# An FFT and a two-layer network in one kernel: the moving operands of both layers read by halves in turn

## The chip, the cores and the metric

The kernel runs on one core of a Trainium2 chip. The metric is the device time of one execution in microseconds. The kernel before takes 1714.6 us, the median of three runs (1714.3 to 1715.34). TensorE (PE in the profile) multiplies: a product streams the columns of its moving operand past weights that were loaded ahead (PEld), and leaves its result in PSUM. VectorE (DVE), ScalarE (ACT) and GpSimd (POOL) do the elementwise work; SyncE (SP) issues the DMAs.

## The reference

```python
X = np.fft.fft(x, axis=1)            # x: (8, 3008, 256) float32
X = np.fft.fft(X, axis=2)
x = X.real.astype(np.float32).reshape(24064, 256)
h = x @ w_in                         # (256, 2048)
r = np.maximum(h, 0.0)
g = s * (r * r) + b
return g @ w_out                     # (2048, 256)
```

## The kernel before, in words

The transform along the sequence is a set of products with cosine and sine tables, folded so that 1506 columns of each of the 8 samples are kept (`NK`), in three blocks of 502 (`NT`, `NBLK`). The transform along the features is folded into the first weights. Every float32 operand of a large product is split into a high part that is rounded to the format `F32R` and a low part, the rest; a product of two operands is then three products: high by high, high by low and low by high.

A step is one block and one group of 128 of the 2048 hidden features, so there are 8 x 3 x 16 = 384 steps.

- `first_layer` (L673) makes the hidden values of a step: for each of two kinds (the even and the odd part in the features) three products of 502 columns, L679, with `spec_h` or `spec_l` as the moving operand, into a PSUM tile `ab` of two banks. VectorE then adds the row `ebc` times `wny` (L681), and forms difference and sum of the two kinds (L682, L683), so that `h` holds the values for a column and for its mirror. ScalarE does the relu (L684) and the square (L685) in place, and rounds to `gh` (L692). GpSimd (in eleven of the first sixteen steps VectorE) forms `gl` = `h` - `gh` (L695).
- `second_layer` (L698) adds a step into the four PSUM banks `po`: for each of the two halves of `h` three products for each of two halves of the 256 outputs, twelve in all, L705, with `gh` or `gl` as the moving operand. In the first block the moving operand has two more columns, which are ones, so that the column sums of `w_out` come out for the bias. `finish` (L708) scales the four banks (L722) and stores them after 16 steps.

So a step has 6 + 12 products of 502 columns, and the kernel 384 x 18 = 6912 of them. Each has its own weights of 128 by 128. The transform's products (L599) and the weights' and edge column's (L338, L478) are the rest of TensorE's work.

The order of the work is written out by hand in two lists of letters, `START` for the beginning and `BATCH` for each later sample: `L` is a `first_layer`, `S` a `second_layer`, the other letters are pieces of loading, transform and weights. `_in_order` holds every engine to the order in which its instructions were written. `spec`, `gh`, `gl` and `h` have three buffers each and `ab` has two.

The order in which a block's 502 columns stand in memory is free: the host gets from `_columns` which column of the output is which, and puts them where they belong.

Of the kernel before, what the change touches and what calls it, by code (L numbers as in the profile page):

```python
# [9 lines left out]
F32 = mybir.dt.float32  # L10
# [3 lines left out]
ALU = mybir.AluOpType  # L14

P = 128
# [8 lines left out]
NT = 502  # L25
NBLK = 3
# [70 lines left out]
def _quarters(ph):  # L97

    m = _residues(ph)
    n = H // 4 if ph else Q // 4  # L100
    return np.stack([m, n - m, 2 * n - m, n + m], axis=1)


def _columns():

    ks, turned = [], []
    for ph in range(2):
        m = _quarters(ph)
        n = H if ph else Q
        both = np.stack([m, n - m], axis=1)  # L110
        sg = np.stack([_SIGMA, -_SIGMA])[None, :, :, None] + 0 * both
        k = both * (1 if ph else 2)
        k, sg = k.reshape(4, 8, G), sg.reshape(4, 8, G)
        if ph == 0:
            parts = [
                (0, lambda v: v.reshape(2, 4 * G)[:, :-1]), (1, lambda v: v.reshape(4, 2 * G)[:, :-1]),
                (2, lambda v: v), (3, lambda v: v[:, :-1]),
            ]
        else:
            parts = [(0, lambda v: v), (3, lambda v: v), (1, lambda v: v[:, :-1]), (2, lambda v: v[:, :-1])]  # L120
        for r, cut in parts:
            ks.append(cut(k[r]).ravel())
            turned.append(cut(sg[r]).ravel() < 0)
    return np.concatenate(ks), np.concatenate(turned)


def _dft_tables():
# [123 lines left out]
def kernel(ctx: ExitStack, tc: tile.TileContext, xq, xn, dft, turn, feat, w_in, w_out, s, b, out):  # L251
    nc = tc.nc
# [14 lines left out]
    def two_banks():  # L267
        return ps_ab.tile([P, 2, 512], F32, name="ab")
# [14 lines left out]
    wny = const.tile([P, NJ], F32, name="wny")  # L283
# [214 lines left out]
    def block_of(su, blk):  # L498
        if (su, blk) not in spec_tiles:
            spec_tiles[su, blk] = [spec.tile([P, 2, NT], F32R, name=f"spec_{part}") for part in "hl"]  # L500
        return spec_tiles[su, blk]
# [168 lines left out]
            yield  # L670


    def first_layer(su, blk, j, ebc):  # L673
        mh, ml = block_of(su, blk)
        ps = two_banks()[:, :, :NT]
        fj = slice(j * P, (j + 1) * P)
        for kind in range(2):
            for i, (w, m) in enumerate(((wd_h, mh), (wd_h, ml), (wd_l, mh))):
                nc.tensor.matmul(ps[:, kind], w[:, kind, fj], m[:, kind], start=i == 0, stop=i == 2)  # L679
        h = act.tile([P, 2, NT], F32, name="h")  # L680
        nc.vector.scalar_tensor_tensor(h[:, 0], ebc, wny[:, j:j + 1], ps[:, 0], op0=ALU.mult, op1=ALU.add)  # L681
        sub(h[:, 1], h[:, 0], ps[:, 1])  # L682
        add(h[:, 0], h[:, 0], ps[:, 1])  # L683
        nc.scalar.activation(h, h, AF.Relu)  # L684
        nc.scalar.activation(h, h, AF.Square)  # L685
        gh = act.tile([P, 2, NT + 2], F32R, name="gh")
        gl = act.tile([P, 2, NT + 2], F32R, name="gl")
        if (su, blk) == (0, 0):

            nc.gpsimd.memset(gh[:, 0, NT:].bitcast(F32), 1.0)  # L690
            nc.gpsimd.memset(gl[:, 0, NT:].bitcast(F32), 0.0)
        nc.scalar.copy(gh[:, :, :NT], h)  # L692
        yield gh, gl
        engine = nc.vector if su == blk == 0 and j in LOWS_OF_STEPS_ON_VECTOR else nc.gpsimd
        engine.tensor_sub(gl[:, :, :NT], h, gh[:, :, :NT].bitcast(F32))  # L695
        yield

    def second_layer(po, j, g, sums):  # L698
        gh, gl = g
        start, stop = j == 0, j == NJ - 1  # L700
        for pm in range(2):
            n = NT + 2 if sums and pm == 0 else NT
            for l, r, first, last in ((wo_h, gh, True, False), (wo_l, gh, False, False), (wo_h, gl, False, True)):
                for dh in range(2):
                    nc.tensor.matmul(  # L705
                        po[2 * pm + dh][:, :n], l[:, j, dh * P:(dh + 1) * P], r[:, pm, :n],
                        start=start and first, stop=stop and last,
                    )  # L708

# [76 lines left out]
    po = None  # L786
    ebc = None
    step = 0

    def first():  # L790
        nonlocal ebc, step
        su, blk, j = step // (NBLK * NJ), step // NJ % NBLK, step % NJ
        step += 1
        if j == 0:
            ebc = small.tile([P, NT], F32, name="ebc")
            for ph in range(2):
                first, last = max(0, blk * NT - SPLIT * ph), min((blk + 1) * NT - SPLIT * ph, e_dram[ph].shape[1])
                if first < last:
                    at = first + SPLIT * ph - blk * NT
                    nc.sync.dma_start(  # L800
                        ebc[:, at:at + last - first], e_dram[ph][su, first:last].partition_broadcast(P)
                    )
        lows.append(first_layer(su, blk, j, ebc))
        pending.append(((su, blk, j), next(lows[-1])))

    def second():
        nonlocal po
        (su, blk, j), g = pending.pop(0)
        if j == 0:
            po = [ps_o.tile([P, 512], F32, name="po") for _ in range(4)]  # L810
        second_layer(po, j, g, (su, blk) == (0, 0))
        if j == NJ - 1:
            finish(su, blk, po)
# [67 lines left out]
```

## Time and profile before

| | |
|---|---|
| median of three runs | 1714.6 us |
| span of the profiled execution, first to last instruction | 1712.9 us |
| TensorE busy | 1674.9 us, 98% of the span |
| VectorE busy | 1403.5 us, 82% |
| ScalarE busy | 1284.6 us, 75% |
| GpSimd busy | 935.4 us, 55% |
| granted TensorE clock, mean of the span | 0.996 of 2.4 GHz |

The profiled execution has no time of its own beside its span; the median of the runs lies 1.7 us above the span, which is what lies around the first and the last instruction. Products are pipelined: the duration that the profile gives for one holds time in which the next already runs, so what one product costs is read from the distance between the starts of successive ones, not from its duration.

### The profile page before, as it was taken

The numbers are of one execution on the slowest core, as the hardware profiler recorded it, in microseconds if no ns is written. First come the engines' busy times: TensorE is split into PE (matmuls) and PEld (weight loads), VectorE is DVE, ScalarE is ACT, GpSimd is POOL, SyncE is SP. The second block draws the span as 40 slices with busy tenths as digits, with TensorE's granted clock in tenths as the row PEclk, the third lists the DMA queues.
The fourth block names the chain that finished last, engine by engine and source line by source line (L and its number), as shares of the span: only waits on it lengthen the run. The fifth ranks groups of instructions, "written<-read, shape, count | busy, mean of one in ns | idle before, by whom it ended". The sixth has DMA issues, their size and how long they took to land.

```text
span 1712.9 us, 21686 instructions
## 1 busy us (share of the span) xinstructions
PE 1674.9 (98%) x7585; PEld 1382.3 (81%) x7585; DVE 1403.5 (82%) x2134; ACT 1284.6 (75%) x1357; POOL 935.4 (55%) x562
## 2 busy tenths in 40 slices
PE   4899999999999999999999999999999999999998
PEld 3678888788888888888888888888888888888887
DVE  7998989898778978799787997879878897875453
ACT  3877777677787777877877778777878777787776
POOL 5645555555555555655556556555565555565554
PEclk9899999999999999999999999999999999999999
DMA  7421201120001100021000200002000110000000
GB/s 184 111 63 59 64 23 31 29 76 31 1 31 53 52 31 2 30 77 29 31 7 34 77 25 25 31 23 73 22 19 30 44 43 31 1 31 30 2 24 25
DMA packets 25570, 68.56 MB, mean 40 GB/s; under 512 B 4915, under 2 KB 9875, under 8 KB 25366
## 3 DMA queue, kind: packets, MB, share of 16 engines
q1 hardware_dynamic: 24934, 64.83, 12.4%
q0 software_dynamic: 528, 2.36, 0.6%
q8 instruction: 59, 0.97, 0.2%
q14 instruction: 49, 0.40, 0.1%
HBM read 42.45 MB, written 24.73 MB: 39 GB/s over the span
## 4 chain that ended last, share of the span: by engine, by line
PE 89%; DVE 6%; ACT 3%; issue 1%; DMA 1%; POOL 0%; SPq 0%; DVEq 0%; ACTq 0%; POOLq 0%
PE po L705 57%; PE ab L679 28%; PE ab L599 3%; DVE h L681 1%; DVE h L682 1%; DMA raw<-in_w_in 1%; DVE h L683 1%; ACT h L685 1%; PE ab L338 1%; ACT h L684 1%; ACT gh L692 1%; DVE xt L512 0%; DVE cs L517 0%; PE ab L478 0%; POOL gl L695 0%
## 5 line engine op out<-in xcount | busy, mean ns | idle before, releaser
L695 POOL TENSOR_TENSOR gl<-h,gh 128x1004 fp32r<-128x1004 f32 x373 | 817.9, 2193 | 707.9 <-ACT gh L692 488.6
L684 ACT ACTIVATE h<-h 128x1004 f32<-128x1004 f32 x384 | 400.3, 1042 | 350.6 <-DVE h L683 336.0
L705 PE MATMUL po<-gh,wo_h 128*128 128x502 f32 (+1 forms) x1536 | 479.9, 393 | 0.3 <-DVE o L722 0.2
L705 PE MATMUL po<-gl,wo_h 128*128 128x502 f32 (+1 forms) x1536 | 475.1, 391 | 0.7 <-POOL gl L695 0.4
L705 PE MATMUL po<-gh,wo_l 128*128 128x502 f32 (+1 forms) x1536 | 475.3, 391 | 0.0
L681 DVE SCALAR_TENSOR_TENSOR h<-ebc,wny,ab 128x502 f32<-128x502 f32 x384 | 281.3, 733 | 234.5 <-PE ab L679 221.8
L685 ACT ACTIVATE h<-h 128x1004 f32<-128x1004 f32 x384 | 401.3, 1045 | 12.2
L692 ACT CAST gh<-h 128x1004 fp32r<-128x1004 f32 x384 | 397.4, 1035 | 12.6 <-PE po L705 0.3
L705 PEld LDWEIGHTS po<-gl,wo_h 128*128 128x128 f32 x1536 | 290.5, 189 | 61.5 <-POOL gl L695 1.7
L705 PEld LDWEIGHTS po<-gh,wo_l 128*128 128x128 f32 x1536 | 289.1, 188 | 61.3
L705 PEld LDWEIGHTS po<-gh,wo_h 128*128 128x128 f32 x1536 | 286.6, 189 | 59.8 <-DVE o L722 2.7
L679 PE MATMUL ab<-spec_h,wd_h 128*128 128x502 f32 x768 | 303.2, 395 | 7.3 <-ACT spec_h L564 3.7
L679 PE MATMUL ab<-spec_h,wd_l 128*128 128x502 f32 x768 | 300.1, 391 | 0.0
L679 PE MATMUL ab<-spec_l,wd_h 128*128 128x502 f32 x768 | 299.2, 390 | 0.0
L683 DVE TENSOR_TENSOR h<-h,ab 128x502 f32<-128x502 f32 x384 | 260.6, 679 | 13.2
L682 DVE TENSOR_TENSOR h<-h,ab 128x502 f32<-128x502 f32 x384 | 260.2, 678 | 13.3
L679 PEld LDWEIGHTS ab<-spec_h,wd_h 128*128 128x128 f32 x768 | 145.8, 190 | 42.8 <-DVE h L683 9.3
L679 PEld LDWEIGHTS ab<-spec_l,wd_h 128*128 128x128 f32 x768 | 145.8, 190 | 29.2 <-POOL spec_l L566 0.5
L679 PEld LDWEIGHTS ab<-spec_h,wd_l 128*128 128x128 f32 x768 | 144.6, 188 | 30.0
L599 PE MATMUL ab<-dft_sb,fh 96*128 96x192 f32 (+1 forms) x288 | 65.8, 306 | 18.3 <-ACT fh L577 18.3
L722 DVE TENSOR_SCALAR o<-po,sb_s,bias 128x502 f32<-128x502 f32 x94 | 68.8, 794 | 10.4 <-PE po L705 10.4
L512 DVE TENSOR_TENSOR xt<-xt 96x512 f32<-96x512 f32 x56 | 73.4, 1311 | 0.0
(103 smaller groups left out, 960.1 us busy)
## 6 DMA issues: line engine op xcount, KB each, us to landing
xt<-in_xq SPq DMA_DIRECT2D x64, 384.0 KB
out<-o SPq DMA_DIRECT2D x46, 502.0 KB
raw<-in_w_in SPq DMA_DIRECT2D x8, 512.0 KB
raw<-in_w_out SPq DMA_DIRECT2D x8, 512.0 KB
ebc<-e_dram SPq DMA_DIRECT2D x16, 251.0 KB
dft_sb<-in_dft POOLq DMA_DIRECT2D x2, 576.0 KB, 10.6
dft_sb<-in_dft POOLq DMA_DIRECT2D x1, 1152.0 KB, 7.2
ebc<-e_dram SPq DMA_DIRECT2D x8, 126.0 KB
```

The costliest lines, as they stand in the source:

```text
L512: add(t[:, 0::2], t[:, 0::2], t[:, 1::2])
L599: nc.tensor.matmul(dst, st, moving, start=n == 0, stop=n == len(work) - 1)
L679: nc.tensor.matmul(ps[:, kind], w[:, kind, fj], m[:, kind], start=i == 0, stop=i == 2)
L681: nc.vector.scalar_tensor_tensor(h[:, 0], ebc, wny[:, j:j + 1], ps[:, 0], op0=ALU.mult, op1=ALU.add)
L682: sub(h[:, 1], h[:, 0], ps[:, 1])
L683: add(h[:, 0], h[:, 0], ps[:, 1])
L684: nc.scalar.activation(h, h, AF.Relu)
L685: nc.scalar.activation(h, h, AF.Square)
L692: nc.scalar.copy(gh[:, :, :NT], h)
L695: engine.tensor_sub(gl[:, :, :NT], h, gh[:, :, :NT].bitcast(F32))
L705: nc.tensor.matmul(po[2 * pm + dh][:, :n], l[:, j, dh * P:(dh + 1) * P], r[:, pm, :n], start=start and first, stop=stop and last,)
L722: nc.vector.tensor_scalar(o[:, dh], po[2 * pm + dh][:, :NT], *args, ALU.mult, ALU.add)
```

## The change

In every product of both layers the moving operand is read as a pattern of 251 pairs: column 0, column 251, column 1, column 252, and so on (`in_turn`), where it was read straight through. The result is written to PSUM without gaps (`beside`), so its columns stand in the order in which they were read. `ebc` is read by VectorE in the same order, so that it meets the right columns. After the first layer the columns have been reordered once; the second layer reads `gh` and `gl` in turn again, so the outputs are reordered twice, and `_columns` turns both back on the host. `gh` and `gl` are now laid out as two halves of 252 places a piece, with 251 values and, in the first block, a one (in `gl` a zero) at the end of each, so that the pair of extra columns is still read last. The two halves stand 1004 bytes apart in `spec_h` and `spec_l`, and 1008 bytes apart in `gh` and `gl`. The rounding to `gh` and the subtraction for `gl` go over four runs of 251 where they went over two of 502. The number of instructions and their order stay the same on every engine; no wait is added or taken away.

```diff
@@ _columns
-    return np.concatenate(ks), np.concatenate(turned)
+    in_turn = np.arange(NT).reshape(2, NT // 2).T.ravel()
+    order = (np.arange(NBLK)[:, None] * NT + in_turn[in_turn]).ravel()
+    return np.concatenate(ks)[order], np.concatenate(turned)[order]
@@ new, ahead of first_layer
+    def in_turn(v, k=2):
+
+        return v.rearrange("p (k n) -> p n k", k=k)
+
+    def beside(v, k=2):
+        return v.rearrange("p (n k) -> p n k", k=k)
@@ first_layer
-                nc.tensor.matmul(ps[:, kind], w[:, kind, fj], m[:, kind], start=i == 0, stop=i == 2)
+                nc.tensor.matmul(
+                    beside(ps[:, kind]), w[:, kind, fj], in_turn(m[:, kind]), start=i == 0, stop=i == 2
+                )
         h = act.tile([P, 2, NT], F32, name="h")
-        nc.vector.scalar_tensor_tensor(h[:, 0], ebc, wny[:, j:j + 1], ps[:, 0], op0=ALU.mult, op1=ALU.add)
+        nc.vector.scalar_tensor_tensor(
+            beside(h[:, 0]), in_turn(ebc), wny[:, j:j + 1], beside(ps[:, 0]), op0=ALU.mult, op1=ALU.add
+        )
...
-            nc.gpsimd.memset(gh[:, 0, NT:].bitcast(F32), 1.0)
-            nc.gpsimd.memset(gl[:, 0, NT:].bitcast(F32), 0.0)
-        nc.scalar.copy(gh[:, :, :NT], h)
+            for t, value in ((gh, 1.0), (gl, 0.0)):
+                nc.gpsimd.memset(t[:, 0].rearrange("p (k n) -> p k n", k=2)[:, :, NT // 2].bitcast(F32), value)
+        gh_halves, gl_halves = (t.rearrange("p m (k n) -> p m k n", k=2)[:, :, :, :NT // 2] for t in (gh, gl))
+        h = h.rearrange("p m (k n) -> p m k n", k=2)
+        nc.scalar.copy(gh_halves, h)
         yield gh, gl
...
-        engine.tensor_sub(gl[:, :, :NT], h, gh[:, :, :NT].bitcast(F32))
+        engine.tensor_sub(gl_halves, h, gh_halves.bitcast(F32))
@@ second_layer
-                        po[2 * pm + dh][:, :n], l[:, j, dh * P:(dh + 1) * P], r[:, pm, :n],
+                        beside(po[2 * pm + dh][:, :n]), l[:, j, dh * P:(dh + 1) * P], in_turn(r[:, pm])[:, :n // 2],
```

## Rows read from the trace of the kernel before

**Rows 1.** The page, busy time by engine (share of the span, instructions)

```profile
PE 1674.9 (98%) x7585; PEld 1382.3 (81%) x7585; DVE 1403.5 (82%) x2134; ACT 1284.6 (75%) x1357; POOL 935.4 (55%) x562
```

**Rows 2.** The page, the chain that ended last, by engine

```profile
PE 89%; DVE 6%; ACT 3%; issue 1%; DMA 1%; POOL 0%; SPq 0%; DVEq 0%; ACTq 0%; POOLq 0%
```

**Rows 3.** Stretches of 200 us: length, busy time of each engine (instructions), clock, DMA

```profile
0.00:200.00 200.00, 168.76 (x774) 132.44 (x775) 175.82 (x295) 138.32 (x186) 106.02 (x138) 0.97 0.36 97
...
400.00:600.00 200.00, 200.00 (x906) 166.42 (x906) 169.06 (x255) 152.34 (x158) 109.70 (x58) 1.00 0.12 36
...
1400.00:1600.00 200.00, 200.00 (x911) 166.58 (x910) 146.92 (x221) 152.05 (x157) 111.20 (x58) 1.00 0.06 20
```

**Rows 4.** Timeline of TensorE, the last 48 second-layer products: start, duration, instructions

```profile
1697.07 0.62 PE L705 MATMUL po<-gh,wo_h 128*128 128x502 f32 x2
...
1707.61 0.62 PE L705 MATMUL po<-gl,wo_h 128*128 128x502 f32 x2
```

**Rows 5.** Timeline of TensorE, twelve first-layer products in a row

```profile
809.01 0.39 PE L679 MATMUL ab<-spec_h,wd_h 128*128 128x502 f32 x1
...
811.75 0.61 PE L705 MATMUL po<-gh,wo_h 128*128 128x502 f32 x2
```

**Rows 6.** Stretches at either clock (columns as in rows 3)

```profile
41.00:46.30 5.30, 5.30 (x7) 2.20 (x8) 5.20 (x9) 1.53 (x3) 2.83 (x4) 0.50 0.33 99
52.40:57.00 4.60, 4.44 (x10) 3.25 (x11) 4.45 (x7) 3.90 (x9) 3.60 (x4) 0.50 0.32 96
73.30:76.80 3.50, 3.50 (x10) 1.59 (x10) 3.43 (x5) 3.44 (x5) 1.93 (x6) 1.00 0.78 194
89.10:92.30 3.20, 3.20 (x47) 2.97 (x45) 3.06 (x6) 3.14 (x4) 2.28 (x6) 1.00 0.00 0
```

**Rows 7.** Timeline of TensorE, first-layer products within the second of these stretches

```profile
53.92 0.62 PE L679 MATMUL ab<-spec_h,wd_l 128*128 128x502 f32 x1
...
56.44 0.62 PE L679 MATMUL ab<-spec_h,wd_l 128*128 128x502 f32 x1
```

**Rows 8.** Timeline of TensorE, weight folding in plain float32, passes of 512 columns

```profile
41.00 6.54 PE L338 MATMUL ab<-cs,feat_sb 128*128 128x512 f32 x8 [1.14 <-DVE wd_l L273]
...
73.35 3.60 PE L338 MATMUL ab<-cs,feat_sb 128*128 128x512 f32 x8
```

**Rows 9.** The same line: durations in ns, minimum, median, maximum

```profile
L338 PE MATMUL ab<-cs,feat_sb x24: 591/592/1192, 41.0 to 113.1; 128*128 128x512 f32 x24
L338 PE MATMUL ab<-aux,feat_sb x8: 592/592/659, 33.1 to 36.2; 128*128 128x512 f32 x8
```

**Rows 10.** Edge-column products with 16 columns of weights: the line, then the timeline

```profile
L478 PE MATMUL ab<-dft_sb,room_r x45: 205/209/337, 89.1 to 92.2; 96*16 96x96 f32 x24, 96*16 96x192 f32 x18, 96*16 96x384 f32 x3
```
```profile
89.09 3.35 PE L478 MATMUL ab<-dft_sb,room_r 96*16 96x384 f32 x45
92.28 0.38 PE L599 MATMUL ab<-dft_sb,fh 96*128 96x96 f32 x2
```

**Rows 11.** L679 alone, then L705 alone, in the first 200 us (columns: PE, PEld)

```profile
0.00:200.00 200.00, 51.38 (x193) 37.02 (x194) 0.97 0.36 97
```
```profile
0.00:200.00 200.00, 84.17 (x348) 65.17 (x348) 0.97 0.36 97
```

**Rows 12.** Groups of instructions on VectorE: busy us, mean ns, idle before

```profile
L681 DVE SCALAR_TENSOR_TENSOR h<-ebc,wny,ab 128x502 f32<-128x502 f32 x384 | 281.3, 733 | 234.5 <-PE ab L679 221.8 <-POOL gl L695 12.2
L683 DVE TENSOR_TENSOR h<-h,ab 128x502 f32<-128x502 f32 x384 | 260.6, 679 | 13.2
...
L514 DVE TENSOR_TENSOR xt<-xt 96x256 f32<-96x256 f32 x56 | 39.3, 702 | 0.0
```

**Rows 13.** L681 alone in a steady stretch (column: DVE)

```profile
400.00:600.00 200.00, 34.43 (x47) 1.00 0.12 36
```

**Rows 14.** Waits: who, for whom, us in total, times, longest

```profile
POOL gl L695 <- ACT gh L692: 488.6, 260, 6.8
ACT h L684 <- DVE h L683: 336.0, 218, 5.9
DVE h L681 <- PE ab L679: 221.8, 142, 4.7
```

**Rows 15.** Groups on ScalarE and GpSimd

```profile
L695 POOL TENSOR_TENSOR gl<-h,gh 128x1004 fp32r<-128x1004 f32 x373 | 817.9, 2193 | 707.9 <-ACT gh L692 488.6 <-DVE h L682 63.5 <-PE po L705 34.5
L685 ACT ACTIVATE h<-h 128x1004 f32<-128x1004 f32 x384 | 401.3, 1045 | 12.2
L692 ACT CAST gh<-h 128x1004 fp32r<-128x1004 f32 x384 | 397.4, 1035 | 12.6 <-PE po L705 0.3
```

## The prediction

> **What bounds the kernel now.** I read the busy times first. TensorE is busy for 98% of the span and no other engine for more than 82% [rows 1], and the chain that ended last runs through TensorE for 89% [rows 2]. The stretches say where that holds: between 400 and 600 us TensorE has no gap at all, and only the first 200 us have waits, 200 − 168.8 = 31.2 us [rows 3]. So from about 200 us on the time is the sum of what TensorE's products take, and the question is what sets the time of one.
>
> A product's cost is the distance between starts. The last second-layer products: 24 rows of two, the first at 1697.07 and the last at 1707.61, so 46 products in 10.54 us, 229.1 ns each [rows 4]. First layer: 12 in 811.75 − 809.01 = 2.74 us, 228.3 ns [rows 5]. I use 228.7. At a full clock of 2.4 GHz 502 columns, one in a cycle, would be 502 / 2.4 = 209.2 ns. A product is thus 19.5 ns late, 9%, with the clock granted in full [rows 3].
>
> What is it late for? Three comparisons. While the clock was at 1.2 GHz [rows 6], six products of the same line took 56.44 − 53.92 = 2.52 us, 420 ns each [rows 7], against 502 / 1.2 = 418.3: nearly nothing lost. Plain float32 passes (32 records for 16 products, so two passes each) started (3.60 − 0.59) / 7 = 430 ns apart at the full clock [rows 6, 8, 9]. That is 512 columns at 0.84 ns, two cycles a column, 426.7, and again nearly nothing lost. The edge-column products at the full clock, whose weights are 16 columns, took 92.28 − 89.09 = 3.19 us for 24 x 96 + 18 x 192 + 3 x 384 = 6912 columns [rows 10], 0.461 ns a column against 0.417. So the loss is there with small weights too, and it is there only when a new column of 4 bytes is called for every 0.417 ns; at one every 0.83 ns it is 2 to 3 ns a product. I read this as a limit on how fast the moving operand reaches the array. The change alters the order of exactly that read.
>
> **The change, part by part.**
>
> *The moving reads.* 6912 products, none added or moved. No row shows a moving operand read in pairs from two places, so I bound it. Low end: one column in a cycle with the 2 ns that the slow-clock row loses, 209.2 + 2 = 211 ns, a gain of 17.7 ns. High end: the slowest that any row shows a column to go is the float32 pass at 1.2 GHz; its eight records took 6.54 us and, the last one's tail of 0.59 us and the clock's return near the end aside, lie about 850 ns apart [rows 6, 8, 9], 1.67 ns a column, which is 837 ns for 502. Between them lies 420 ns, a column every 0.83 ns. Which? By turns, each of the two halves is called for one column every 0.83 ns, and each half is read straight through. A stream of 4-byte columns at 0.83 ns is what rows 7 and 8 show to run without loss, and two such streams make the rate that one stream misses by 9%. If the two halves are served apart, the product takes 211 ns; that is the value I take. If they share one path that gains from neighbours, it goes towards 420 or above. This is a choice between ends far apart, and the chances say so.
>
> Of the 6912 products 193 + 348 = 541 lie in the first 200 us [rows 11]; the other 6371 stand back to back. 6371 x 17.7 ns = 112.8 us. The early ones are worth 541 x 17.7 = 9.6 us, but TensorE waits there for other engines, so I count a third, 3 us.
>
> *The row `ebc`.* L681 reads `ebc` in pairs. It takes 733 ns for 502 columns now, and its neighbour L683, which reads nothing in pairs, 679 [rows 12]. Low end 0. High end: the slowest VectorE row per element of like kind, 256 elements in 702 ns, 2.74 ns each, which would be 1377 ns, 644 more [rows 12]. I take 0, since L681 itself is the nearest row, and VectorE has 200 − 169 = 31 us of slack in a steady 200 us [rows 3], in which 47 of L681 stand [rows 13]. At the high end 47 x 0.644 = 30 us would use all of it.
>
> *Rounding and subtraction over four runs.* L692 over two runs takes 1035 ns, L685 over one run of the same 1004 elements 1045 [rows 15]: a further run costs nothing that shows. GpSimd takes 2193 ns for `gl` and is busy 55%, mostly waiting for L692 [rows 14, 15]. Low and high end 0 and, by a tenth of 2193, 220 ns that its waits cover. I take 0. The memsets are as many as before, in the first block only.
>
> *What is late next.* If TensorE does 200 us of work in 200 x 211 / 228.7 = 184.5 (the transform's few products included, which is a little too good), VectorE's 169 becomes 92% of the stretch, ScalarE's 152 becomes 83% [rows 3]. Now L681 waits for TensorE (221.8 us in all) and ScalarE for VectorE (336.0) [rows 14]; with less slack some of these waits turn round and TensorE waits for `ab`. In 1400 to 1600 us VectorE has only 147 [rows 3], so nothing is lost there. I take 15 us as given back.
>
> Sum against the span: 1712.9 − 112.8 − 3 + 15 = 1612.1. The median lies 1.7 us above the span: 1614 us.
>
> **A rule of the Trainium skill that speaks against it.** What the rows show is a loss that appears with the rate of 4-byte columns [rows 4, 7, 8]. The Trainium skill ("Advanced Engine Details and Errata", section "SBUF Cachelines") says that the memory is read in lines of 16 bytes, that at least two accesses in a row should hit a line to cover its latency, and that an access to a different line each time is penalised. Straight through, four columns share a line; by turns, no two successive ones do. The page gives no size for the penalty; no run here yet shows it on TensorE. By that rule the time is that of the first rival.
>
> **The rivals.**
>
> 1. *Every column becomes an access of its own, and a product runs at one column every 0.83 ns.* Slower. The place is L679 and L705 after 55 us, the price 420 − 228.7 = 191 ns a product [rows 4, 7], and it decides as soon as a product takes more than 229 ns, since no gap of TensorE is left to take it. 6912 x 191 = 1320 us, of which the early waits absorb perhaps 20: 1715 + 1300 = 3015 us. For it: pairs from two places lose all neighbourhood. Against it: each half alone is straight, at a rate that rows 7 and 8 show to be easy. At the high bound of 837 ns it would be 1715 + 6912 x 0.608 = 5917 us.
> 2. *Nothing changes.* If the 9% belongs to the bytes a cycle brings, wherever they lie, a product stays at 228.7 and the time at 1715. For it: the loss per column is alike in the lines of 502 columns and in short ones [rows 4, 10]. Against it: something must make a read fall behind, and the order of addresses is the first thing that could.
> 3. *VectorE becomes the bound.* L681 at 1377 ns brings a steady stretch to 199 of 200 us. With TensorE unchanged, hiccups of some 2% make 1735 to 1750; with TensorE faster, VectorE holds the six stretches between 200 and 1400 us at their present time, and only the last 313 us shrink by 8%, 24 us: 1690.
> 4. *In between.* A product at 240 to 380 ns, if pairs lose only part: 1800 to 2760.
>
> **How the numbers follow.** Chances: forecast 0.52 (with the faster case of the third rival in it), 3015 us or so 0.21, nothing changes 0.12, VectorE slower 0.08, in between 0.04, beyond half rate 0.03. The likeliest has its own range from 1592 (no give-back and all early gains: 1714.6 − 122.4) to 1690. The whole range must leave out no more than 0.2, and without the first rival 0.28 would be left out, so it reaches to 3040; its low end is 1590. A change within 0.2%, 3.4 us, can't be told from none. Faster 0.52, same 0.12, slower 0.36.
>
> **What would show it.** Right: the last 48 products of L705 start 211 ns apart (46 in 9.7 us), L679 likewise, the granted clock still 1.00, TensorE without gaps in steady stretches, VectorE over 90% there and L681 still near 733 ns. Wrong: products 229 ns apart (second rival), or 400 and more with VectorE and ScalarE near half idle (first), or L681 well over 1 us with TensorE waiting for VectorE's L683 (third). The give-back is wrong if TensorE shows no idle time, or more than 30 us, after 200 us.

## The result, and the profile after

The changed kernel takes 1675.6 us (1674.8 to 1676.4), the kernel before 1714.9 us: a ratio of 0.977, 95% interval 0.9757 to 0.9785. That is 39 us faster, where 101 were forecast. The rest of this document is about the 62 that are missing. In the changed kernel L679 is L688, L681 to L683 are L692, L695 and L696, L684 and L692 are L697 and L707, L695 is L710, and L705 is L720.

The products do what was forecast. This is TensorE's timeline after, second-layer products near the end that follow each other without a wait (start in us, duration, instructions):

```profile
1658.88 0.58 PE L720 MATMUL po<-gh,wo_h 128*128 128x502 f32 x2
...
1664.38 0.59 PE L720 MATMUL po<-gh,wo_l 128*128 128x502 f32 x2
```

Fourteen rows of two, so 26 products in 5.50 us: 211.5 ns each, where it was 229.1 [rows 4]. The first layer runs at the same pace: three products of L688 ahead of one of L720 take 0.64 us, 213 ns each.

```profile
830.08 0.38 PE L688 MATMUL ab<-spec_h,wd_h 128*128 128x502 f32 x1
830.29 0.38 PE L688 MATMUL ab<-spec_l,wd_h 128*128 128x502 f32 x1
830.51 0.37 PE L688 MATMUL ab<-spec_h,wd_l 128*128 128x502 f32 x1
830.72 0.58 PE L720 MATMUL po<-gh,wo_h 128*128 128x502 f32 x2
```

But TensorE no longer stands full. First the page's busy times and chain, then the stretches (length, busy time of PE, PEld, DVE, ACT and POOL with instructions, clock, DMA):

```profile
PE 1589.0 (95%) x7585; PEld 1381.3 (82%) x7585; DVE 1425.3 (85%) x2134; ACT 1278.0 (76%) x1357; POOL 926.8 (55%) x562
...
PE 51%; DVE 33%; ACT 8%; issue 5%; POOL 2%; DMA 1%; SPq 0%; POOLq 0%; DVEq 0%; ACTq 0%
```
```profile
0.00:200.00 200.00, 163.75 (x777) 132.16 (x778) 176.39 (x295) 138.53 (x186) 105.00 (x138) 0.98 0.37 98
...
400.00:600.00 200.00, 192.99 (x929) 169.41 (x930) 177.53 (x262) 155.27 (x161) 111.76 (x58) 1.00 0.12 36
...
1400.00:1600.00 200.00, 196.34 (x937) 173.44 (x936) 145.46 (x215) 157.92 (x162) 113.27 (x60) 0.99 0.05 20
```

Beside [rows 1 to 3]: TensorE's share falls from 98% to 95%, and the chain, which ran 89% through TensorE, runs 51% through it and 33% through VectorE. Between 400 and 600 us TensorE had no gap; now it has 7 us of them, and 929 instructions fit where 906 did, not the 976 or so that 211.8 ns a product in place of 228.1 (the means that follow) would allow. Who holds it up stands in the waits (who, for whom: us in total, times, longest):

```profile
ACT h L697 <- DVE h L696: 308.9, 186, 5.7
DVE h L692 <- PE ab L688: 155.7, 95, 4.2
PE ab L688 <- DVE h L696: 42.0, 45, 2.4
```

The last line has grown from 3.5 us in the trace before: TensorE wants a buffer `ab` that VectorE's third operation of a step has not yet left. VectorE's own wait for TensorE shrank from 221.8 to 155.7 us [rows 14]. The reads in pairs cost VectorE nothing (L692; busy, mean, idle before), as against 733 [rows 12]:

```profile
L692 DVE SCALAR_TENSOR_TENSOR h<-ebc,wny,ab 128x502 f32<-128x502 f32 x384 | 280.7, 731 | 177.5 <-PE ab L688 155.7 <-POOL spec_l L568 13.7 <-POOL gl L710 8.2
```

**The account.** I summed the distances between the starts of all TensorE instructions after 200 us, in both traces. An undisturbed product went from 228.1 to 211.8 ns, and some 6370 products stand there: 104 us gained. Products that had to wait lost 9.1 us beyond their own time before and 65.0 after: 56 back. Products in stretches in which the clock was at 1.2 GHz lost 0 and 8.3. The transform's products lost 1.8 more. 104 − 56 − 8 − 2 = 38, the difference of the spans (1712.9 − 1674.6). The first 200 us gave 0.6.

The loss has an address. The starts of the same products in the two traces, three steps (54 products) at a time, in one sample (a sample is 48 steps, and the others read alike):

```
from step     before: us for three steps     after
   114               12.29                    11.44
   117               12.29                    11.43
   120               13.20                    14.24
   123               13.18                    16.64
   126               12.35                    11.43
   ...
   153               12.31                    11.43
   156               12.32                    13.79
   159               12.68                    11.72
   162               12.29                    11.44
```

Nearly everywhere three steps gain 0.7 to 0.9 us; at steps 120 to 125 and 156 to 158 they lose 1 to 3.5. The same place one sample on (steps 168 to 173) in VectorE's timeline after:

```profile
792.41 0.55 DVE L608 COPY t<-ab 128x384 f32<-128x384 f32 x1
792.99 0.55 DVE L609 TENSOR_TENSOR t<-t,ab 128x384 f32<-128x384 f32 x1
793.58 1.59 DVE L613 TENSOR_TENSOR x<-t 128x384 f32<-128x384 f32 x1
795.10 0.55 DVE L614 TENSOR_TENSOR x<-t 128x384 f32<-128x384 f32 x1
795.68 0.69 DVE L388 TENSOR_TENSOR uv<-cs 96x512 f32<-96x512 f32 x1
796.29 2.62 DVE L389 TENSOR_TENSOR uv<-cs 96x512 f32<-96x512 f32 x1
798.84 0.72 DVE L692 SCALAR_TENSOR_TENSOR h<-ebc,wny,ab 128x502 f32<-128x502 f32 x1
799.59 0.68 DVE L695 TENSOR_TENSOR h<-h,ab 128x502 f32<-128x502 f32 x1
800.31 0.68 DVE L696 TENSOR_TENSOR h<-h,ab 128x502 f32<-128x502 f32 x1
```

Six operations of the transform stand ahead of a step's three. One of them, L389, takes 2.62 us, because GpSimd has just begun its `gl`; in the trace before the same operation, L387, came at another moment and took 0.68:

```profile
795.89 2.47 POOL L710 TENSOR_TENSOR gl<-h,gh 128x1004 fp32r<-128x1004 f32 x1 [1.13 <-ACT gh L707]
```
```profile
810.62 0.69 DVE L386 TENSOR_TENSOR uv<-cs 96x512 f32<-96x512 f32 x1
811.23 0.68 DVE L387 TENSOR_TENSOR uv<-cs 96x512 f32<-96x512 f32 x1
811.83 0.73 DVE L681 SCALAR_TENSOR_TENSOR h<-ebc,wny,ab 128x502 f32<-128x502 f32 x1
```
```profile
811.25 2.69 POOL L695 TENSOR_TENSOR gl<-h,gh 128x1004 fp32r<-128x1004 f32 x1 [1.54 <-ACT gh L692]
```

Before, VectorE began 0.02 us ahead of GpSimd (811.23 and 811.25), and it was GpSimd's operation that took longer; after, GpSimd began 0.40 us ahead. The meeting costs VectorE 2.62 − 0.68 = 1.94 us, and TensorE's wait behind it is 2.39 us (next fence): of this wait some 0.45 us would be left without the meeting, by this difference, which is an estimate.

TensorE waits until 801.13 and, soon after, runs at half speed for a while (its timeline, then the stretch):

```profile
801.13 0.45 PE L688 MATMUL ab<-spec_h,wd_h 128*128 128x502 f32 x1 [2.39 <-DVE h L696]
...
802.92 1.04 PE L720 MATMUL po<-gh,wo_h 128*128 128x502 f32 x2
803.76 1.04 PE L720 MATMUL po<-gh,wo_l 128*128 128x502 f32 x2
804.59 1.00 PE L720 MATMUL po<-gl,wo_h 128*128 128x502 f32 x2
```
```profile
802.00:805.40 3.40, 3.40 (x10) 2.72 (x9) 2.62 (x6) 3.34 (x5) 1.02 (x1) 0.50 0.31 59
```

There the granted clock is 0.50, and four products take 1.67 us, 418 ns each. Five such stretches stand in the trace between 200 and 1600 us, a sample apart, each behind this wait; a sixth wait of the same length, which ended at 400.06, has none behind it. Before there were none.

At steps 156 to 158 VectorE meets GpSimd's `gl` as well: L515 and L519, 0.41 to 0.42 us otherwise, take 2.25 and 2.36 us.

```profile
722.90 2.25 DVE L515 TENSOR_TENSOR xt<-xt 96x256 f32<-96x256 f32 x1
...
725.87 2.36 DVE L519 TENSOR_TENSOR cs<-xt 96x256 f32<-96x256 f32 x1
```

Such meetings are not new as such (in the trace before, an L512 at 736.74 took 1.90 us for 0.68 to 0.74), and one that was there before can begin to cost: an operation of 2.27 us ahead of steps 168 to 170 took 2.29 before, and TensorE waits 0.86 us behind it only now.

### The profile page after: what moved, and what is told of

Read it like the earlier page. It is cut to its first block, busy times and chain, and to the rows that moved or that the text cites. A ratio compares the mean times of both kernels' runs of the same rounds, so it can differ in the third digit from the quotient of the medians.

```text
span 1674.6 us, 22015 instructions
## 1 busy us (share of the span) xinstructions
PE 1589.0 (95%) x7585; PEld 1381.3 (82%) x7585; DVE 1425.3 (85%) x2134; ACT 1278.0 (76%) x1357; POOL 926.8 (55%) x562
## 3 DMA queue, kind: packets, MB, share of 16 engines
q0 software_dynamic: 528, 2.36, 0.6%
## 4 chain that ended last, share of the span: by engine, by line
PE 51%; DVE 33%; ACT 8%; issue 5%; POOL 2%; DMA 1%; SPq 0%; POOLq 0%; DVEq 0%; ACTq 0%
PE po L720 32%; PE ab L688 16%; DVE h L695 5%; DVE h L692 5%; DVE h L696 5%; ACT h L698 2%; ACT h L697 2%; PE ab L601 2%; DVE xt L514 2%; ACT gh L707 2%; DVE lf L370 2%; DVE xt L515 2%; POOL gl L710 2%; DVE t L614 1%; DVE cs L519 1%
## 5 line engine op out<-in xcount | busy, mean ns | idle before, releaser
L710 POOL TENSOR_TENSOR gl<-h,gh 128x1004 fp32r<-128x1004 f32 x373 | 810.6, 2173 | 677.5 <-ACT gh L707 550.3
L697 ACT ACTIVATE h<-h 128x1004 f32<-128x1004 f32 x384 | 398.9, 1039 | 318.9 <-DVE h L696 308.9
L720 PE MATMUL po<-gh,wo_h 128*128 128x502 f32 (+1 forms) x1536 | 459.3, 380 | 0.0
L720 PE MATMUL po<-gl,wo_h 128*128 128x502 f32 (+1 forms) x1536 | 454.1, 377 | 3.1 <-POOL gl L710 2.4
L720 PE MATMUL po<-gh,wo_l 128*128 128x502 f32 (+1 forms) x1536 | 453.0, 377 | 0.0
L692 DVE SCALAR_TENSOR_TENSOR h<-ebc,wny,ab 128x502 f32<-128x502 f32 x384 | 280.7, 731 | 177.5 <-PE ab L688 155.7
L707 ACT CAST gh<-h 128x1004 fp32r<-128x1004 f32 x384 | 395.3, 1029 | 12.3
L688 PE MATMUL ab<-spec_h,wd_h 128*128 128x502 f32 x768 | 295.2, 384 | 46.4 <-DVE h L696 42.0
L720 PEld LDWEIGHTS po<-gl,wo_h 128*128 128x128 f32 x1536 | 290.9, 190 | 42.2 <-POOL gl L710 5.7
L720 PEld LDWEIGHTS po<-gh,wo_h 128*128 128x128 f32 x1536 | 288.6, 190 | 43.1 <-DVE o L737 6.6
L720 PEld LDWEIGHTS po<-gh,wo_l 128*128 128x128 f32 x1536 | 291.6, 190 | 34.6
L688 PE MATMUL ab<-spec_l,wd_h 128*128 128x502 f32 x768 | 290.6, 378 | 0.3 <-POOL spec_l L568 0.3
L688 PE MATMUL ab<-spec_h,wd_l 128*128 128x502 f32 x768 | 289.1, 376 | 0.0
L696 DVE TENSOR_TENSOR h<-h,ab 128x502 f32<-128x502 f32 x384 | 260.4, 678 | 13.2
L695 DVE TENSOR_TENSOR h<-h,ab 128x502 f32<-128x502 f32 x384 | 260.2, 678 | 13.3
L688 PEld LDWEIGHTS ab<-spec_h,wd_h 128*128 128x128 f32 x768 | 144.8, 189 | 86.1 <-issue 28.2
L688 PEld LDWEIGHTS ab<-spec_h,wd_l 128*128 128x128 f32 x768 | 146.3, 191 | 17.6
L688 PEld LDWEIGHTS ab<-spec_l,wd_h 128*128 128x128 f32 x768 | 145.2, 189 | 16.4 <-POOL spec_l L568 0.6
L601 PEld LDWEIGHTS ab<-dft_sb,fh 96*128 96x128 f32 x288 | 54.6, 199 | 28.6 <-ACT fh L579 20.0
```

What stands on the lines that cost most here:

```text
L601: nc.tensor.matmul(dst, st, moving, start=n == 0, stop=n == len(work) - 1)
L688: nc.tensor.matmul(beside(ps[:, kind]), w[:, kind, fj], in_turn(m[:, kind]), start=i == 0, stop=i == 2)
L692: nc.vector.scalar_tensor_tensor(beside(h[:, 0]), in_turn(ebc), wny[:, j:j + 1], beside(ps[:, 0]), op0=ALU.mult, op1=ALU.add)
L707: nc.scalar.copy(gh_halves, h)
L710: engine.tensor_sub(gl_halves, h, gh_halves.bitcast(F32))
L720: nc.tensor.matmul(beside(po[2 * pm + dh][:, :n]), l[:, j, dh * P:(dh + 1) * P], in_turn(r[:, pm])[:, :n // 2], start=start and first, sto ...
```

## The experiments

**Each layer alone.** The change in one layer, the other as before; the host turns back once.

```diff
@@ first layer alone, against the changed kernel
-                        beside(po[2 * pm + dh][:, :n]), l[:, j, dh * P:(dh + 1) * P], in_turn(r[:, pm])[:, :n // 2],
+                        po[2 * pm + dh][:, :n], l[:, j, dh * P:(dh + 1) * P], r[:, pm, :n],
...
@@ second layer alone, against the changed kernel
-                    beside(ps[:, kind]), w[:, kind, fj], in_turn(m[:, kind]), start=i == 0, stop=i == 2
+                    ps[:, kind], w[:, kind, fj], m[:, kind], start=i == 0, stop=i == 2
```

> Only the first layer reads its halves by turns (2304 of 6912 products). If the pace of a product depends on its own read alone, L688 runs at 212 ns and L720 stays at 228; the gain of 2304 x 16.9 = 39 us is given back in part only, since VectorE still has slack: about 1684 us. The rival, that a fixed share of every gain is lost (38 of 117 us kept when both layers turn), gives 1715 - 13 = 1702 us.

> Only the second layer reads by turns (4608 of 6912 products). L705 at 212 ns, L679 at 228. If VectorE is what gives the gain back, 4608 x 16.9 = 78 us are gained and some 40 given back, close to what both layers together reach: about 1678 us. The rival of a fixed share gives 1715 - 25 = 1690 us.

First layer alone: 1709.8 us against 1714.0 (ratio 0.9975, 0.9966 to 0.9984). Second layer alone: 1685.6 (0.9825, 0.9809 to 0.9842). In both the pace of a product depends on its own read alone, as expected: the median distance is 212 ns behind the turned products and 229 behind the others. The times fell out otherwise. Of 2304 x 16.3 = 38 us the first layer keeps 4, and of 4608 x 16.3 = 75 the second keeps 28. My 1684 and 1678 were too low, and the rival's 1702 and 1690 missed too, one low and one high. So the give-back does not wait until some spare is used up: it comes in with the first few per cent of pace. The place is the same. At steps 123 to 125, 13.18 us before, three steps take 14.96 with the first layer alone and 15.01 with the second alone. What stands there does not get shorter when TensorE gets faster, and gets longer by the collision: L389 takes 2.62 to 2.66 us at this place in both, and TensorE's wait behind it, 1.8 to 2.0 us, is about what the meeting costs VectorE.

**VectorE's work taken away.** Samples 2 to 7 compute with the folded data of sample 1 again, in the changed kernel and in the one before.

```diff
+        if su > 1:
+            folded[su] = folded[1]
+            for _ in range(16):
+                yield
+            return
         cs = fold.tile([P, 2, 8, 2 * P], F32, name="cs")
```

> The changed kernel without the loading and folding of samples 2 to 7 (they compute with the folded data of sample 1 again), so 48 x 5 of VectorE's instructions of lines 514 to 519 are gone, some 185 us of its 1425. If VectorE's load is what gives the gain back, TensorE's waits after 200 us (some 56 us more than before) and the drops of its clock (8 us) nearly vanish: 1610 to 1625 us, products still 212 ns apart. The rival, that the two ab buffers and the chain through ScalarE hold TensorE whatever VectorE has to do, expects 1655 us or more.

> The kernel before with the same loading and folding left out. TensorE has no gap in its steady stretches, so taking VectorE's work away gives nothing there: 1705 to 1714 us by either theory. If it came to 1690 or less, VectorE (or the DMA of the samples) would have cost time before the change already.

1639.1 us (0.956, 0.9532 to 0.9588) and 1711.9 (0.9983, 0.9972 to 0.9994). The same work, taken away, is worth 36 us after the change and 3 before it: VectorE was no limit, and is one now. (The transfers of these samples go with it; but what TensorE waited for in the changed kernel was above all VectorE's L696, 42.0 us.) 1639 lies below the 1655 of the rival, but above the 1610 to 1625 that I expected. Steps 156 to 158 are cured (11.43 us), steps 123 to 125 are not (14.63 in place of 16.64), though VectorE has only 154 of 200 us to do in a steady stretch:

```profile
400.00:600.00 200.00, 196.67 (x954) 174.14 (x953) 154.21 (x226) 158.99 (x164) 113.78 (x60) 1.00 0.05 20
```

So it is not VectorE's sum of work that decides but where it stands, and what it meets there: at steps 123 to 125 L389 still takes 2.64 us, and TensorE waits 2.06 us behind it. No stretch at 1.2 GHz is left after 200 us in this trace.

**Another order.** The same 138 letters of `BATCH`, with the pieces of loading and transform spread out.

```diff
-    "L l S L L S l S L l l S L l l S l L S l L S L S l L l L S S L S l L l S L l S S L l L l S L v l S L S v S L "
-    "L S L v S v L v v v S L v L v S L S S L S L S L S L v S L S v L S v L v o S L S L L o S S L o o S o o S L o "
-    "S L o L S o L S L S L S L S L S o o L S L S L S L o o S L S"
+    "L S l L S L l l S L l l S l L S L S l S L l L S l L l L S S L S L l L l S S l S l L L l S S L L S l S v L L v "
+    "S L v v S v L v v L S L v S L v S L S v L L S S L S L v S L S v L L S v o S L v S L L S o L S o o o o L S L S S "
+    "o L L S o L L S o L S S o L o S L S L S L L S o S L o S"
```

> The changed kernel with another BATCH: the same 138 letters, with the pieces of loading and transform spread out, so that VectorE's work no longer piles up at one place of a sample; no work left out, the result put back as in the changed kernel. If the gain was lost where VectorE's transform pieces pile up (some 9 us a sample at steps 120 to 126 and their like), most of it comes back: 1615 to 1635 us, with products still 212 ns apart. If VectorE's sum of work is the limit (175 to 187 of 200 us), order changes little: 1660 us or more.

> The kernel before with the same new BATCH. Its TensorE had no gaps in the steady stretches, so by the theory of the pile nothing is to be had: 1708 to 1716 us. If the new order were better in itself, for whatever reason, it would show here as well: 1690 us or less.

With the change 1636.9 us against 1715.5 (0.9541, 0.9527 to 0.9555), and without it 1726.4 (1.0061, 1.0045 to 1.0078). The new order gives 39 us back to the changed kernel and costs the old one 11. It lies 2 us above the range that I gave for the pile and far from the 1660 of the rival; the old kernel's 1726 lies above my 1708 to 1716. Steps 123 to 125 take 11.95 us; VectorE still has 171 of 200 us to do, 169 before the change and 178 with it:

```profile
400.00:600.00 200.00, 197.69 (x956) 174.70 (x956) 171.13 (x267) 160.32 (x167) 115.56 (x60) 1.00 0.12 37
```

This version beats both kernels. Some 22 us of waits more than before the change are left in it, 2.6 of them in each sample at steps 159 to 161, where the old kernel with this order loses too (13.87 us for 12.68).

The new order takes away the pile and the meeting at once. The same operation in the changed kernel, with VectorE's work taken away, and with the new order (durations in ns, minimum, median, maximum):

```profile
L389 DVE TENSOR_TENSOR uv<-cs x8: 676/2622/2628, 33.9 to 1400.4; 96x512 f32<-96x512 f32 x8
L389 DVE TENSOR_TENSOR uv<-cs x8: 676/2641/2653, 33.5 to 1364.8; 96x512 f32<-96x512 f32 x8
L389 DVE TENSOR_TENSOR uv<-cs x8: 676/682/683, 34.0 to 1366.0; 96x512 f32<-96x512 f32 x8
```

VectorE is busy for 1364.7 us in all with the new order, 1425.3 without it, with as many instructions. That the loss hangs on the order is shown; how much of it is the pile and how much the meetings with GpSimd no run separates. At steps 120 to 125 the durations speak for the meeting.

**Why turns help.** In the kernel before, the second layer reads its columns in four other orders.

```diff
@@ the first probe: quarters by turns (line 707), even columns and then odd ones (line 709)
+                    if pm == 0:
+                        nc.tensor.matmul(out.rearrange("p (n k) -> p n k", k=4), weights, moving.rearrange("p (k n) -> p n k", k=4), **flags)
+                    else:
+                        nc.tensor.matmul(out.rearrange("p (k n) -> p k n", k=2), weights, moving.rearrange("p (n k) -> p k n", k=2), **flags)
...
@@ the second probe: 0 4 1 5 2 6 3 7 (line 707), 0 2 1 3 (line 709); n is 4 in the one and 2 in the other
+    ... moving.rearrange("p (g k n) -> p g n k", n=4, k=2)
```

> The columns of the second layer are left in another order (the output is not put back), and it reads 504 columns in every block. The first half of a step (line 707) reads four quarters by turns, the second half (line 709) all even columns and then all odd ones; the first layer reads straight through. Theory one, that every second column has a reader of its own, which does best when its own columns lie side by side: quarters by turns make each reader jump between two places, and even-then-odd gives each a step of 16 bytes, so both are slower than straight, 250 ns or more, perhaps 420. Theory two, that it is enough that successive columns lie in different places: quarters 212 ns, even-then-odd 229 ns or more. The rule of lines of 16 bytes with two hits in a row: quarters slow, even-then-odd 229 ns.

> The columns of the second layer are left in another order (the output is not put back), and it reads 504 columns in every block. The first half of a step (line 707) reads in the order 0 4 1 5 2 6 3 7 of every eight columns, so turns between two neighbouring pieces of 16 bytes; the second half (line 709) in the order 0 2 1 3 of every four, so turns within one piece. Theory one (a reader for every second column) and theory two (successive columns in different places) both expect 212 ns for line 707 and 229 ns for line 709. If the halves have to be far apart, line 707 stays at 229 ns; if any turn is enough, both run at 212 ns.

TensorE's timeline of the first probe, then of the second:

```profile
1002.94 0.70 PE L707 MATMUL po<-gh,wo_h 128*128 128x504 f32 x2
1003.47 0.70 PE L707 MATMUL po<-gh,wo_l 128*128 128x504 f32 x2
1004.01 0.70 PE L707 MATMUL po<-gl,wo_h 128*128 128x504 f32 x2
1004.54 1.06 PE L709 MATMUL po<-gh,wo_h 128*128 128x504 f32 x2
1005.42 1.07 PE L709 MATMUL po<-gh,wo_l 128*128 128x504 f32 x2
```
```profile
1002.90 0.59 PE L707 MATMUL po<-gh,wo_h 128*128 128x504 f32 x2
1003.33 0.59 PE L707 MATMUL po<-gh,wo_l 128*128 128x504 f32 x2
1003.75 0.59 PE L707 MATMUL po<-gl,wo_h 128*128 128x504 f32 x2
1004.18 0.63 PE L709 MATMUL po<-gh,wo_h 128*128 128x504 f32 x2
1004.64 0.61 PE L709 MATMUL po<-gh,wo_l 128*128 128x504 f32 x2
```

Two products of 504 columns take from one row's start to the next. A product, in each order (502 columns in the first two rows of the table, 504 in the others):

| order of columns | ns a product (medians over the run, by place in a step) |
|---|---|
| straight (the kernel before) | 229 |
| two halves by turns (the change) | 212 |
| 0 4 1 5 2 6 3 7 | 212 |
| 0 2 1 3 | 226 to 233 |
| four quarters by turns | 263 to 268 |
| even columns, then odd ones | 436 to 447 |

Theory one passes all four: what counts is what every second column of the order sees. Where its own columns lie side by side (halves, and 0 1 2 3 beside 4 5 6 7) a product takes 212; where it gets two of every four neighbours (straight, and 0 2 1 3) 226 to 233; where each lies 16 bytes on from the last, 445. The halves needn't be far apart: 16 bytes do. Theory two fell with the quarters (268 where it said 212). The readers themselves were not seen; they are inferred from six orders. That quarters cost 268 and not 445, though each reader's next column is always far off, is left open. Time as a whole: 2310 us for the first probe and 1719 for the second, one run each.

## Why the prediction was right or wrong

**What bounds the kernel: right.** The moving operand's way to the array was the limit that cost a product 9%, and the order of addresses moved it.

**The choice of 211 ns: right, and for its reason.** I chose the low end since each half by itself is called at a pace that the rows showed to be easy. The probes bear that out: each second column of the order is served apart. The gain per product was 16.3 ns and not 17.7, 104 us after 200 us where I had 112.8.

**The rule of the Trainium skill: not as I read it.** By turns no two successive columns share 16 bytes, and the product got faster; even columns first, where two successive ones do share them, took 445 ns. The Trainium skill ("Advanced Engine Details and Errata", section "SBUF Cachelines") asks for at least two accesses to a line in a row. Applied to every second column, the rule has the right direction: four in a row 212 ns, two 229, one 445; the quarters, one in a row as well, lie between at 268. But two in a row, which by the rule are enough, still lose 17 ns here. So the first rival, built on the whole sequence, was wrong, and gave the range its high end of 3040 for nothing.

**The cost of `ebc`, rounding and subtraction: right.** `ebc` is read at 731 ns an operation, 733 before; the rounding takes 1029 for 1035 and the subtraction 2173 for 2193.

**The step that failed: "I take 15 us as given back."** Measured: 66 us (56 of waits, 8 of clock, 2 in the transform). I took VectorE's mean over a steady stretch, 169 of 200 us, scaled it to 92% and gave a guess for the hiccups. After, it was 89%, and the loss was four times the guess. The mean could not tell it: even between 1400 and 1600 us, where VectorE had 147 of 200 us to do and I expected no loss, TensorE stood still for 3.7 us. VectorE's work of the transform and the folding stands at a few places of each sample, up to ten operations in a row between the steps' own, and the order there was as tight as TensorE at 229 ns just allowed: VectorE ran without a gap there, and TensorE had no wait. A faster TensorE shifts the engines against each other. At steps 123 to 125 this makes an operation of VectorE start behind GpSimd's `gl`, where it had started 0.02 us ahead of it, and the 1.9 us that it then takes longer are most of TensorE's wait of 2.4 us; with either layer alone, where three steps lose 1.8 us, they are nearly all of it. How the rest of the 56 us divides between the tight order and such meetings stays open. The third rival had the right engine, but the wrong mechanism (a dearer L681) and, for its faster case, 1690 us.

**What was not in the sum at all:** VectorE operations that meet GpSimd's `gl` at another moment (2.62 us for 0.68), and the clock that falls behind the new wait.

**The first 200 us:** 0.6 us for 3. There the waits for other engines took nearly all.

## What to carry to other kernels

When one engine is to be made faster in a schedule that was written out for its old pace, don't compare the others' mean load with the new pace: go through a period step by step and look for the place where another engine's queue is full, since the gain is lost there however idle that engine is elsewhere. Look also for operations of two engines that get in each other's way: at the new pace they meet at other moments. Then order anew: the same reordering was worth 39 us to the changed kernel and cost the old one 11. A stream that falls a few per cent short of one column in a cycle, at full clock and with no gap, is worth a try of other address orders; a probe with several orders in one kernel shows in one trace which of them is fast.

## What the runs showed of the hardware

- A moving operand of 4-byte columns, read straight through at 2.4 GHz, takes mostly 221 to 233 ns for 502 columns; read by turns from two places, 210 to 213, one column in a cycle (209.2) and 2 to 3 ns more in the mean (211.8). In these runs the two places lay 16 bytes apart (504 columns, 212 ns) or about 1000 bytes.
- 504 columns read at a step of 8 bytes take 436 to 447 ns, and read from four places by turns 263 to 268.
- A VectorE subtraction of two operands in SBUF that starts just after GpSimd's 2.1 us subtraction took 2.62 us in place of 0.68: it ended 0.55 us after GpSimd's did (795.89 + 2.47 = 798.36 to 798.91); so did, within 0.01 us, all 24 such meetings of this line after 200 us in the changed kernel, in the two with one layer changed and in the one with VectorE's work left out, with GpSimd 0.03 to 0.40 us ahead. Where VectorE began 0.02 us ahead, it took its 0.68 us, and GpSimd's 2.69.
- Behind a wait of TensorE of 2.4 us the granted clock fell to 1.2 GHz for 3.4 us, at 600.6, 802.0, 1003.4, 1204.8 and 1406.2 us; behind the same wait that ended at 400.06 it did not. With one layer changed it fell behind two of six such waits (1.8 to 2.0 us) in either kernel.
